# The first batch's attention norms by exp(ln(x)/2) from column sums held in every partition, scores scaled from PSUM in one pass, and v loaded behind the first weights

## The chip, the cores and the metric

The kernel runs on one core of a Trainium2 chip. The metric is the device time of one execution in microseconds. The kernel before took 830.83 us (median). TensorE is PE in the profile (PEld its weight loads), VectorE is DVE, ScalarE is ACT, GpSimd is POOL, SyncE is SP. SBUF and PSUM are the core's on-chip memories: in this kernel the tiles named ps_ lie in PSUM, the others in SBUF, and an "eviction" copies a matmul's result from a ps_ tile to SBUF.

## The reference

Four batches of cross-covariance attention over 6016 rows of 256 channels, and a gated feed-forward layer over all 24064 rows:

```python
qn = q / (norm(q, axis=1) + 1e-6);  kn = k / (norm(k, axis=1) + 1e-6)
a  = softmax(kn.T @ qn / tau)                     # 256 x 256 per batch, tau = 1
x  = (v @ a)                                      # 24064 x 256
out = (sigmoid(x @ w_gate) * (x @ w_val)) @ w_out # 256 -> 1536 -> 256
```

The kernel multiplies a into the weights first ("products" below: G = a·w_gate, H = a·w_val, twelve pieces of 128 x 512), so the large part of the work is v·G, v·H, their GLU (sigmoid of the gate half times the value half) and the product with w_out.

## The kernel before

For the first batch it streams q and k in, multiplies them into scores on TensorE, and sums squares for the norms. Then comes a stretch in which nothing large can run: norms, softmax, first products, first GLU step. This is the part that the change and the argument touch, with cuts (filler matmuls and arguments left out):

```python
for g, (t0, nt) in enumerate(groups0):      # stream of q and k
    ...                                     # squares, scores, norm sums as 4 columns
    norm_mms(ps_n0, ...)                    # sum of squares: q's 256 and k's 256 channels
norms_sqrt(0)                               # ScalarE: Sqrt of 128x4
nc.scalar.preload_act_table(ACT.Exp)
copy_s(0, 0); norms_inv(0); copy_s(0, 1)    # VectorE: +1e-6, reciprocal of 128x4; scores to SBUF
spread_k(0, 0, ...); spread_k(0, 1, ...)    # TensorE: k's inverse norms into every partition
weights(0, 0); weights(0, 1)                # VectorE product, ScalarE exponential, per 128x128
transpose_v(0, 0, ...)                      # first v group, TensorE, copied by VectorE and ScalarE
sums(0, 0); gh(0, 0, act=False); gh(0, 1, act=True)   # row sums; products, evicted by VectorE / ScalarE
sums(0, 1); gh(0, 2, act=False); gh(0, 3, act=True)
nc.scalar.preload_act_table(ACT.Sigmoid)
gh(0, 4, act=False)
# main loop: glu(b, ci, f), out_mms(...); side work in fixed slots, e.g.
at(7, lambda: transpose_v(0, 1, ...))       # second v group
```

Engines run their instructions in the order in which the program gives them. Later batches already compute their norms from k's sums in every partition, with a wide reciprocal, but beside the GLU of the batch before, where nobody waits for them.

Of the kernel before, what the change touches and what calls it, by code (L numbers as in the profile page):

```python
# [8 lines left out]

FP32 = mybir.dt.float32  # L10
BF16 = mybir.dt.bfloat16
# [6 lines left out]
def kernel(  # L18
# [20 lines left out]
    nc = tc.nc  # L39
# [47 lines left out]
    def mm(out, lhsT, rhs, start, stop, **kw):  # L87
        nc.tensor.matmul(out, lhsT=lhsT, rhs=rhs, start=start, stop=stop, **kw)  # L88
# [23 lines left out]
    first_f32 = [consts.tile([P, nt, C], FP32, name=f"first{w}") for w in range(2)]  # L112
    for eng, tl, src in zip((nc.sync, nc.scalar), first_f32, (q, k)):
        eng.dma_start(out=tl, in_=rows(src, 0)[:, t0 : t0 + nt, :])
    nc.scalar.preload_act_table(ACT.Sqrt)
    load_qk(0, *groups0[1])

    ident_bf = consts.tile([P, P], BF16)
    make_identity(nc, ident_bf)
    ident_f = consts.tile([P, P], FP32)  # L120
    make_identity(nc, ident_f)
    ones_bf = consts.tile([P, P], BF16)
    nc.vector.memset(ones_bf, 1.0)
    ones_wide = consts.tile([P, CH], BF16)
# [5 lines left out]
    nc.scalar.copy(qk[0, 0][1], first_f32[1])  # L130
    for t0, nt in groups0[2:]:
        load_qk(0, t0, nt)
    load_v(0, 0)

    w_sb = [[consts.tile([P, CB, FG], BF16, name=f"w_{n}{fg}") for fg in range(NFG)] for n in ("gate", "val")]
    w_out_sb = consts.tile([P, FC, C], BF16)
    for fg in range(NFG):
        for w, src in enumerate((moe_w_gate, moe_w_val)):
            nc.gpsimd.dma_start(  # L139
                out=w_sb[w][fg],  # L140
                in_=src.rearrange("(t p) f -> p t f", p=P)[:, :, ds(fg * FG, FG)],
            )
    load_v(0, 1)
    nc.gpsimd.dma_start(out=w_out_sb, in_=moe_w_out.rearrange("(t p) c -> p t c", p=P))

# [32 lines left out]
            )  # L178
        return sq

    def norm_mms(ps, sqs, nt, first, last, order=(0, 1)):

        for w in order:
            sq = sqs[w]
            for u in range(nt):
                for j in range(CB):
                    mm(
                        ps[:, w * CB + j : w * CB + j + 1],
                        sq[:, u, ds(j * P, P)],
                        ones_bf[:, 0:1],  # L190
                        start=(first and w == order[0] and u == 0 and j == 0),
                        stop=(last and u == nt - 1),
                        skip_group_check=True,
                    )

    def acc_start(b):
        st.setdefault(b, {})["acc"] = [
# [38 lines left out]
    def norms_mm(b):  # L236

        s = st[b]
        fold_q, fold_k = s["fold"]
        ps = psm.tile([P, CB + C], FP32, tag="m", name="ps_n")  # L240
        norm_mms(ps, (fold_q,), 2, True, True, (0,))
        for u in range(2):
            mm(ps[:, CB:], ones_bf, fold_k[:, u, :], False, u == 1, skip_group_check=True)
        s["n"] = ps

    def wide_sqrt(b):
# [25 lines left out]
                op1=ALU.mult,  # L272
            )

    def norms_sqrt(b):
        s = st[b]
        s["r"] = attp.tile([P, 2 * CB], FP32, tag="r", name="r")
        nc.scalar.activation(out=s["r"], in_=s["n"], func=ACT.Sqrt)

    def norms_inv(b):  # L280
        r = st[b]["r"]
        nc.vector.tensor_scalar(out=r, in0=r, scalar1=1e-6, scalar2=None, op0=ALU.add)
        nc.vector.reciprocal(r, r)
        if inv_tau != 1.0:
            nc.vector.tensor_scalar(
                out=r[:, :CB], in0=r[:, :CB], scalar1=inv_tau, scalar2=None, op0=ALU.mult
            )

    def spread_k(b, i, pl, tag):

        s = st[b]
        ps = pl.tile([P, P], FP32, tag=tag, name="ps_rk")
        mm(ps, s["r"][:, CB + i : CB + i + 1].to_broadcast([P, P]), ident_f, True, True)
        s.setdefault("rk", []).append(ps)

    def copy_s(b, j):
        s = st[b]
        if j == 0:
            s["x"] = attp.tile([P, CB, C], FP32, tag="x", name="x_sb")
        nc.vector.tensor_copy(out=s["x"][:, j, :], in_=s["s"][:, j, :])  # L300

    def weights(b, i):

        s = st[b]
        e = attp.tile([P, CB, P], BF16, tag=f"e{i}", name=f"e_sb{i}", bufs=2)
        for j in range(CB):
            y = attp.tile([P, P], FP32, tag=f"y{i}{j}", name="y_sb")
            nc.vector.tensor_tensor(
                out=y, in0=s["x"][:, j, ds(i * P, P)], in1=s["rk"][i], op=ALU.mult
            )  # L310
            nc.scalar.activation(
                out=e[:, j, :], in_=y, func=ACT.Exp, bias=shift, scale=s["r"][:, j : j + 1]
            )
        s.setdefault("e", []).append(e)
        s.setdefault("rrow", [])

# [39 lines left out]
            for n in ("G", "H")  # L356
        ]

    gh_order = [(fg, w, i) for fg in range(NFG) for i in range(CB) for w in range(2)]

    def gh(b, n, pl=None, tag=None, act=None):
        s = st[b]
# [17 lines left out]

    vts = {}

    def transpose_v(b, ci, ps=None, late=None):

        t0, nt = groups[ci]
        v_sb = vs.pop((b, ci))
        vT = vtpool.tile([P, TPC * CB, P], BF16, tag="vT", name="vT")
        flat = v_sb[:, :nt, :].rearrange("p t c -> p (t c)")
        if ps is None:
            nc.sync.dma_start_transpose(out=vT[:, : nt * CB, :], in_=flat)  # L390
        else:
            for n in range(nt * CB):
                nc.tensor.transpose(
                    out=ps[:, n, :], in_=flat[:, ds(n * P, P)], identity=ident_bf
                )
            half = nt * CB // 2
            nc.vector.tensor_copy(out=vT[:, :half, :], in_=ps[:, :half, :])
            (nc.scalar.copy if late is None else late)(vT[:, half : nt * CB, :], ps[:, half : nt * CB, :])
        vts[b, ci] = vT.rearrange("p (u cb) n -> p cb u n", cb=CB)

    hts = {}
# [70 lines left out]
            mm(ps, ones_bf, ones_wide, True, True)  # L472

    busy(9)
    ps_n0 = psm.tile([P, 2 * CB], FP32, tag="m", name="ps_n")

    n_acc = NT // TPC - 2
    acc_start(0)
# [2 lines left out]
    for g, (t0, nt) in enumerate(groups0):  # L481
        engines = (nc.vector, nc.scalar) if g < last0 else (nc.scalar, nc.vector)
        sq = [squares(0, t0, nt, w, engines[w], acc[w] if g == 0 else None) for w in range(2)]
        if 0 < g < n_acc:
            for w in range(2):
                nc.vector.tensor_tensor(out=acc[w], in0=acc[w], in1=sq[w], op=ALU.add)  # L486
        for u in range(nt):
            score(0, t0, u)
        if g < n_acc:
            busy(5)  # L490
        elif g == n_acc:
            norm_mms(ps_n0, acc, TPC, True, False)
            norm_mms(ps_n0, sq, nt, False, False)
        elif nt == TPC:
            busy(2)
            norm_mms(ps_n0, sq, nt, False, False)
        elif g < last0:
            held = (sq, nt)
        else:
            norm_mms(ps_n0, *held, False, False)  # L500
            norm_mms(ps_n0, sq, nt, False, True, (1, 0))
    st[0]["n"] = ps_n0
    norms_sqrt(0)
    nc.scalar.preload_act_table(ACT.Exp)
    copy_s(0, 0)
    norms_inv(0)
    copy_s(0, 1)
    busy(3)
    spread_k(0, 0, pso, "o")
    spread_k(0, 1, pso, "o")  # L510
    busy(1)
    weights(0, 0)
    weights(0, 1)
    late = []
    transpose_v(
        0, 0, psv.tile([P, TPC * CB, P], BF16, tag="v", name="ps_tp"), lambda *a: late.append(a)
    )
    nc.scalar.copy(*late.pop())
    gh_tiles(0)
    sums(0, 0)  # L520
    gh(0, 0, psg, "g", act=False)
    gh(0, 1, psv, "v", act=True)
    sums(0, 1, pss, "s")
    gh(0, 2, psg, "g", act=False)
    gh(0, 3, psv, "v", act=True)
    nc.scalar.preload_act_table(ACT.Sigmoid)
    gh(0, 4, pso, "o", act=False)


    def side_work(b):  # L530
# [7 lines left out]
        for ci in range(NCH):  # L538
            nb, nci = (b, ci + 1) if ci + 1 < NCH else (b + 1, 0)
            lb, lci = (b, ci + 2) if ci + 2 < NCH else (b + 1, ci + 2 - NCH)  # L540
            if (nb, nci) == (0, 1):
                at(7, lambda: transpose_v(0, 1, psm.tile([P, TPC * CB, P], BF16, tag="m", name="ps_tp")))
            elif nb < B:
                at(ci * FC + 2, transpose_v, nb, nci)
            if lb < B:
                at(ci * FC + 0, load_v, lb, lci)
# [33 lines left out]
    for b in range(B):  # L580
        side = side_work(b)
        for ci in range(NCH):
            block = b + 1 < B and ci in (9, 10)
            for f in range(FC):
                glu(b, ci, f)
                flush()
                if prev is not None and not block:
                    out_mms(*prev, f * TPC, (f + 1) * TPC)
                for fn, a in side.get((ci, f), ()):
                    fn(*a)  # L590
                if (b, ci) == (0, 0) and f < len(gh_order) - 5:
                    gh(0, 5 + f, pso, "o")
            if prev is not None and block:
                for s in range(TPC):
                    for fn, a in side.get((ci, FC + s), ()):
                        fn(*a)
                    out_mms(*prev, s * FC, (s + 1) * FC)
                    flush()
            prev = (b, ci)
# [39 lines left out]
```

## Time and profile before

| Kernel before | |
|---|---|
| time, median of 6 runs | 830.83 us (830.62 to 831.15) |
| span of the profiled run | 829.2 us |
| TensorE busy, 0 to 60 us | 16.01 + 16.30 + 19.08 of 60 us |
| first GLU step's matmuls | start 39.22 us |
| first product with w_out | starts 55.46 us |

The last two rows serve as marks below: from the first product with w_out on, TensorE has the same work in both kernels and hardly ever waits, so a difference at that mark should reappear at the end. In TensorE's timeline the mark is this line:

```profile
55.46 0.60 PE L88 MATMUL ps_o<-w_out_sb,hT 128*128 128x256 bf16 x4
```

The stretch between the last norm sum and the first exponentials, which the change replaces, reads as follows in ScalarE's and then VectorE's timeline of the kernel before (start us, length us, engine, line, operation, out<-in; in brackets the idle time before it and what ended it):

```profile
34.47 0.17 ACT L278 ACTIVATE r<-ps_n 128x4 f32<-128x4 f32 x1 [0.49 <-PE ps_n L88]
34.66 1.28 ACT L504 ACT_TABLE_LOAD   x1
36.02 1.65 ACT L311 ACTIVATE e_sb<-y_sb,shift,r 128x128 bf16<-128x128 f32 x4
...
34.87 0.18 DVE L283 RECIPROCAL r<-r 128x4 f32<-128x4 f32 x1
```

The reciprocal is of four columns (0.18 us), and the table load ends at 35.94.

### The profile page before, as it was taken

To read this page: it belongs to the slowest core of one execution; us is meant where nothing else is said; L and a number is where in the kernel's file an instruction comes from. 1 tells how busy PE (TensorE), PEld (TensorE's weight loads), DVE (VectorE), ACT (ScalarE), POOL (GpSimd) and SP (SyncE) were. 2 spreads that over 40 slices of the span, in tenths; PEclk is the share of its full clock that TensorE was granted. 3 is DMA by queue.
4 is the path that set the end of the run, shared out by engine and by line. 5 is a ranking of instruction groups with operands and counts; after the bars stand their busy time and mean duration, and the time that the engine had idled before them with its cause. 6 is when DMAs were issued, how large, how long until landed. Compare 5 with 4: busy or idle time off the path is not lost.

```text
span 829.2 us, 13794 instructions
## 1 busy us (share of the span) xinstructions
PE 816.6 (98%) x5204; PEld 502.9 (61%) x5218; DVE 588.7 (71%) x1023; ACT 391.6 (47%) x644; POOL 83.0 (10%) x159
## 2 busy tenths in 40 slices
PE   7899999999999999999999999999999999999998
PEld 4546666665666666665575666666566566666666
DVE  6577878787667777778767777777766666666665
ACT  4654444446644444445654444444655444444442
POOL 5532100002110100000211010000000000000000
PEclk9999999999999999999999999999999999999999
DMA  9999623226946433223875352223323423322111
GB/s 210 207 206 208 111 52 81 58 63 125 164 81 130 96 79 65 59 52 78 162 140 121 80 108 62 51 54 85 64 54 63 79 52 82 71 49 67 48 36 72
DMA packets 79028, 77.19 MB, mean 93 GB/s; under 512 B 50801, under 2 KB 55921, under 8 KB 78961
## 3 DMA queue, kind: packets, MB, share of 16 engines
q0 software_dynamic: 23920, 38.81, 28.1%
q1 hardware_dynamic: 54752, 36.91, 17.8%
q8 instruction: 41, 0.67, 0.3%
q10 hardware_dynamic: 288, 0.59, 0.2%
q14 instruction: 27, 0.21, 0.1%
HBM read 78.64 MB, written 24.64 MB: 125 GB/s over the span
## 4 chain that ended last, share of the span: by engine, by line
PE 94%; DMA 4%; DVE 1%; issue 0%; POOL 0%; ACT 0%; POOLq 0%; ACTq 0%
PE ps_o L88 30%; PE ps_gate L88 29%; PE ps_val L88 29%; PE ps_s L88 4%; DMA k_sb<-in_k_dram 3%; PE ps_gh L88 2%; DMA w_val<-in_moe_w_val_dram 1%; DVE hT L423 0%; ACT g_sb L422 0%; DVE sq L176 0%; PE ps_end L88 0%; POOL q_sb L97 0%; PE ps_n L88 0%; POOL w_gate L139 0%; POOL k_sb L97 0%
## 5 line engine op out<-in xcount | busy, mean ns | idle before, releaser
L423 DVE TENSOR_TENSOR hT<-ps_val,g_sb 128x512 bf16<-128x512 f32 (+1 forms) x576 | 390.9, 679 | 207.0 <-ACT g_sb L422 202.6
L422 ACT ACTIVATE g_sb<-ps_gate 128x512 bf16<-128x512 f32 (+1 forms) x576 | 338.2, 588 | 386.3 <-PE ps_gate L88 380.3
L88 PE MATMUL ps_gate<-vT,gh_G 128*128 128x512 bf16 (+1 forms) x1152 | 337.7, 375 | 0.6 <-ACT g_sb L422 0.4
L88 PE MATMUL ps_val<-vT,gh_H 128*128 128x512 bf16 (+1 forms) x1152 | 337.5, 375 | 0.4
L88 PE MATMUL ps_o<-w_out_sb,hT 128*128 128x256 bf16 x2244 | 324.8, 273 | 0.0
L88 PEld LDWEIGHTS <-hT 128*128 128x128 bf16 x2268 | 221.0, 98 | 124.6
L88 PEld LDWEIGHTS <-gh_H 128*128 128x128 bf16 x1152 | 112.7, 98 | 131.7 <-issue 1.4
L88 PEld LDWEIGHTS <-gh_G 128*128 128x128 bf16 x1152 | 112.4, 98 | 38.3 <-issue 0.6
L106 POOL DMA_DIRECT2D v_sb<-in_v_dram x48 | 25.5, 531 | 620.6 <-DMA vT<-v_sb 489.7
L449 DVE COPY out_sb<-ps_o 128x256 f32<-128x256 f32 x187 | 77.3, 413 | 12.6 <-PE ps_o L88 12.6
L88 PE MATMUL ps_s<-k_sb,q_sb 128*128 128x256 bf16 x376 | 66.0, 272 | 5.5 <-DMA k_sb<-in_k_dram 4.4
L88 PEld LDWEIGHTS <-q_sb 128*128 128x128 bf16 x376 | 36.6, 98 | 14.1 <-issue 6.8
L215 DVE TENSOR_TENSOR acc<-acc,sq 128x1024 bf16<-128x1024 bf16 (+1 forms) x66 | 44.1, 669 | 0.0
L176 DVE TENSOR_TENSOR sq<-q_sb 128x1024 bf16<-128x1024 bf16 (+2 forms) x44 | 29.4, 667 | 2.7 <-DMA q_sb<-in_q_dram 2.7
L97 POOL DMA_DIRECT2D q_sb<-in_q_dram x48 | 26.4, 551 | 16.5 <-DMA q_sb<-in_q_dram 8.3
L97 POOL DMA_DIRECT2D k_sb<-in_k_dram x48 | 26.3, 547 | 16.1 <-DMA k_sb<-in_k_dram 8.4
L176 DVE TENSOR_TENSOR sq<-k_sb 128x1024 bf16<-128x1024 bf16 (+2 forms) x34 | 22.4, 658 | 0.8 <-ACT sq L174 0.8
L376 ACT ACTIVATE gh_G<-ps_gh,rrow 128x512 bf16<-128x512 f32 x21 | 14.4, 687 | 12.9 <-PE ps_gh L88 9.1
L88 PE MATMUL ps_busy<-ones_wide,ones_bf 128*128 128x512 bf16 x57 | 16.6, 418 | 1.7 <-DVE shift L127 1.6
L174 ACT ACTIVATE sq<-k_sb 128x1024 bf16<-128x1024 bf16 (+1 forms) x11 | 11.2, 1018 | 14.7 <-DMA k_sb<-in_k_dram 11.9
L378 DVE TENSOR_SCALAR gh_H<-ps_gh,rrow 128x512 bf16<-128x512 f32 x22 | 16.3, 743 | 1.6 <-PE ps_gh L88 1.6
L486 DVE TENSOR_TENSOR acc<-acc,sq 128x1024 bf16<-128x1024 bf16 x16 | 11.1, 692 | 5.7 <-ACT sq L174 5.4
(67 smaller groups left out, 126.4 us busy)
## 6 DMA issues: line engine op xcount, KB each, us to landing
out_dram<-out_sb SPq DMA_DIRECT2D x44, 512.0 KB, 2.9
v_sb<-in_v_dram POOLq DMA_DIRECT2D x44, 256.0 KB, 3.8
q_sb<-in_q_dram POOLq DMA_DIRECT2D x43, 256.0 KB, 7.2
k_sb<-in_k_dram POOLq DMA_DIRECT2D x43, 256.0 KB, 8.1
out_dram<-out_sb SPq DMA_DIRECT2D x3, 384.0 KB, 2.5
w_gate<-in_moe_w_gate_dram POOLq DMA_DIRECT2D x3, 256.0 KB, 6.8
w_val<-in_moe_w_val_dram POOLq DMA_DIRECT2D x3, 256.0 KB, 8.1
w_out_sb<-in_moe_w_out_dram POOLq DMA_DIRECT2D x1, 768.0 KB, 12.7
```

What stands on the lines that cost most here:

```text
L88: nc.tensor.matmul(out, lhsT=lhsT, rhs=rhs, start=start, stop=stop, **kw)
L97: nc.gpsimd.dma_start(out=tl[:, :nt, :], in_=rows(src, b)[:, t0 : t0 + nt, :])
L106: nc.gpsimd.dma_start(out=v_sb[:, :nt, :], in_=rows(v, b)[:, t0 : t0 + nt, :])
L174: nc.scalar.activation(out=sq[:, :nt, :], in_=src[:, :nt, :], func=ACT.Square)
L176: engine.tensor_tensor(out=sq[:, :nt, :], in0=src[:, :nt, :], in1=src[:, :nt, :], op=ALU.mult)
L215: nc.vector.tensor_tensor(out=acc[:, :nt, :], in0=acc[:, :nt, :], in1=st[b]["sq", w][:, :nt, :], op=ALU.add)
L376: nc.scalar.activation(out=dst, in_=ps, func=ACT.Copy, scale=r)
L378: nc.vector.tensor_scalar(out=dst, in0=ps, scalar1=r, scalar2=None, op0=ALU.mult)
L422: nc.scalar.activation(out=g_sb[:, :n], in_=ps_gate[:, :n], func=ACT.Sigmoid)
L423: nc.vector.tensor_tensor(out=hts[b, ci][:, f, :n], in0=ps_val[:, :n], in1=g_sb[:, :n], op=ALU.mult)
L449: nc.vector.tensor_copy(out=out_sb[:, s, :], in_=ps)
L486: nc.vector.tensor_tensor(out=acc[w], in0=acc[w], in1=sq[w], op=ALU.add)
```

## The change

The intent is to shorten this stretch: one table set holds ln and exp, so the load between Sqrt and Exp falls away; the norms of k arrive already spread over all partitions, so the spreading matmuls fall away; the scores are scaled directly from PSUM. Along with it, the first v group is loaded behind the first weights, six products instead of five precede the main loop, the first transposes move behind two products, and the second transposes one slot (one step of the main loop) later with ScalarE's copy first. Later batches keep Sqrt. The core of the diff, with cuts and shortened lines:

```diff
-    nc.scalar.preload_act_table(ACT.Sqrt)
+    nc.scalar.add_instruction(mybir.InstLoadActFuncSet(...
+            act_func_set_id=list(get_activation_tables("trn2")).index("natural_log_exp_and_others")))
-    ident_f = consts.tile([P, P], FP32)
-    make_identity(nc, ident_f)
-    load_v(0, 0)
+        if fg == 0:                  # in the loop that loads the weights
+            load_v(0, 0)
     ...
+    def norm_k(ps, sq, nt, last, parts=1):      # k's sums: ones as weights, 256 columns
+                mm(ps[:, CB + i * n : CB + (i + 1) * n], ones_bf, sq[:, u, ds(i * n, n)], ...)
+    def roots(b, part):
+        nc.scalar.activation(out=x, in_=s["n"][:, cols], func=ACT.Ln)
+        nc.scalar.activation(out=x, in_=x, func=ACT.Exp, scale=0.5)
+    def weights(b, i):
+        wide_inv(b, i)                          # + 1e-6, reciprocal, of 130 or 128 columns
+        for j in range(CB):
+            nc.vector.scalar_tensor_tensor(out=y[:, j, :], in0=s["s"][:, j, ds(i * P, P)],
+                scalar=s["r"][:, j : j + 1], in1=s["rk"][:, ds(i * P, P)], op0=ALU.mult, op1=ALU.mult)
+        nc.scalar.activation(out=e, in_=y, func=ACT.Exp, bias=shift)
     ...
-    gh_order = [(fg, w, i) for fg in range(NFG) for i in range(CB) for w in range(2)]
+    gh_order = [(0, w, i) for i in range(CB) for w in range(2)]
+    gh_order += [(fg, w, i) for fg in range(1, NFG) for w in range(2) for i in range(CB)]
     ...
+            nc.scalar.copy(vT[:, half : nt * CB, :], ps[:, half : nt * CB, :])
             nc.vector.tensor_copy(out=vT[:, :half, :], in_=ps[:, :half, :])
-            (nc.scalar.copy if late is None else late)(vT[...], ps[...])
     ...
-    norms_sqrt(0) ... copy_s, norms_inv, spread_k, busy(3), busy(1), transpose_v(0, 0, ...)
+    for i in range(CB):
+        roots(0, i)
+    busy(8)
+    for i in range(CB):
+        weights(0, i)
     gh_tiles(0)
     sums(0, 0)
     gh(0, 0, psg, "g", act=False)
     gh(0, 1, psv, "v", act=True)
+    transpose_v(0, 0, psv.tile([P, TPC * CB, P], BF16, tag="v", name="ps_tp"))
     sums(0, 1, pss, "s")
     ...
     gh(0, 4, pso, "o", act=False)
+    gh(0, 5, pso, "o", act=False)
     ...
-                at(7, lambda: transpose_v(0, 1, ...))
+                at(8, lambda: transpose_v(0, 1, ...))
```

`busy(n)` is n filler matmuls that nobody reads; they keep TensorE working.

## The prediction

> **What bounds the kernel now.** I read the page first, then the busy time by stretches, the chain of work that ended last, the timeline of 28 to 54 us engine by engine, and the groups by form. The page says what fills the span:
>
> ```profile
> PE 816.6 (98%) x5204; PEld 502.9 (61%) x5218; DVE 588.7 (71%) x1023; ACT 391.6 (47%) x644; POOL 83.0 (10%) x159
> ...
> PE 94%; DMA 4%; DVE 1%; issue 0%; POOL 0%; ACT 0%; POOLq 0%; ACTq 0%
> ```
>
> TensorE carries 94% of the chain; everything else together is 6%. The busy time by stretches (columns: length, then busy us and count of PE, PEld, DVE, ACT, POOL, then clock, DMA share, GB/s) shows where that 6% lies:
>
> ```profile
> 0.00:20.00 20.00, 16.01 (x86) 8.95 (x88) 11.96 (x21) 8.67 (x8) 11.29 (x27) 1.00 1.00 210
> 20.00:40.00 20.00, 16.30 (x155) 10.34 (x157) 12.91 (x30) 11.42 (x17) 10.79 (x18) 1.00 1.18 206
> 40.00:60.00 20.00, 19.08 (x101) 9.52 (x101) 13.05 (x22) 12.63 (x21) 6.87 (x13) 1.00 1.20 206
> 60.00:70.00 10.00, 10.00 (x67) 6.29 (x66) 7.24 (x13) 4.18 (x7) 3.70 (x7) 1.00 1.13 197
> ```
>
> From 60 us on TensorE is simply full. Before that it isn't, and the DMA engines are saturated at a constant 206 to 210 GB/s. The change touches only this opening: the first batch's norms and softmax, the first loads, and two transposes of v. So whatever it does is decided before about 54 us, and every us by which TensorE reaches its full stretch earlier or later goes one to one into the end. Two stalls are left there, both seen in TensorE's timeline:
>
> ```profile
> 39.22 0.73 PE L88 MATMUL ps_gate<-vT,gh_G 128*128 128x512 bf16 x2
> 39.78 0.59 PE L88 MATMUL ps_val<-vT,gh_H 128*128 128x512 bf16 x2
> 40.75 0.59 PE L88 MATMUL ps_gh<-w_val,e_sb 128*128 128x512 bf16 x2 [0.37 <-DMA w_val<-in_moe_w_val_dram]
> ...
> 51.62 0.59 PE L88 MATMUL ps_val<-vT,gh_H 128*128 128x512 bf16 x2
> 52.58 0.59 PE L88 MATMUL ps_gate<-vT,gh_G 128*128 128x512 bf16 x2 [0.36 <-ACT g_sb L422]
> 53.31 0.59 PE L88 MATMUL ps_val<-vT,gh_H 128*128 128x512 bf16 x2
> ```
>
> Two 512-column matmuls take one step of 0.43 us (the starts lie that far apart when nothing waits). At 40.75 the sixth product with the weights waits for w_val of the second column group. After 51.62 + 0.43 = 52.05 two further pairs should have ended at 52.91; they end at 53.31 + 0.43 = 53.74, a loss of **0.83 us**. ScalarE's timeline has its cause:
>
> ```profile
> 51.44 0.58 ACT L398 COPY vT<-ps_tp 128x512 bf16<-128x512 bf16 x1 [1.19 <-DVE vT L397]
> 51.92 1.09 ACT L422 ACTIVATE g_sb<-ps_gate 128x512 bf16<-128x512 f32 x2
> ```
>
> ScalarE stood idle for 1.19 us until VectorE had copied its half of the transposed v, and the sigmoids queued behind.
>
> **What the Trainium skill says.** "ScalarE: Activation LUTs", section "Table sets: the hidden batching unit", states that natural_log_exp_and_others holds both exp and ln, so one load serves both; the change relies on it. Section "What ACT_TABLE_LOAD costs" gives about 1283 ns for a load and 186 ns + 0.833 ns per column for an activation without pointer operands. The trace agrees: loads last 1.28 us, and Sqrt of 128x258 took 388 ns against 401 by the formula. (The page adds a drain of about 1380 ns; here Sqrt ended at 34.64 and the load began at 34.66, so I don't count it.) "VectorE: DVE Perf Modes", section "First, the fixed hardware budget", says that Reciprocal is an iterative divide with a repeat count of 8. The trace agrees that it is slow per column, in the later batches, whose norms already have the wide form:
>
> ```profile
> L256 DVE RECIPROCAL n_sb<-n_sb 128x130 f32<-128x130 f32 x3 | 2.9, 966 | 0.1
> L256 DVE RECIPROCAL n_sb<-n_sb 128x128 f32<-128x128 f32 x3 | 2.9, 953 | 0.1
> L321 ACT ACTIVATE e_sb<-x_sb,shift 128x256 bf16<-128x256 f32 x6 | 2.7, 500 | 0.7 <-DVE x_sb L266 0.7
> L266 DVE SCALAR_TENSOR_TENSOR x_sb<-ps_s,n_sb 128x256 f32<-128x256 f32 x6 | 2.6, 474 | 0.0
> ...
> L283 DVE RECIPROCAL r<-r 128x4 f32<-128x4 f32 x1 | 0.2, 178 | 0.0
> ```
>
> "PSUM — Partial Sum Buffer", section "PSUM bank collisions raise a hardware error", says accesses of two engines to one bank must be guarded by bank, reads against reads too. The wait of ScalarE's copy above fits that: its half is another column range of the same tile.
>
> **The change part by part.** *Transfers.* The stream to the last k is the same bytes; the last k lands at 27.11 + 6.5 = 33.6 us as before. v and the first two weight tiles only swap places. Removing the second identity lets GpSimd issue about half a us earlier at 3 us, but the DMA engines are full from there on: 0. The second w_val still lands at 40.7, and the new order asks for it after six products and two GLU steps, so the 0.37 us wait goes, provided the rest isn't later anyway.
>
> *Norm sums.* In the last full group 8 one-column matmuls (16 take 33.34 - 32.93 = 0.41 us, so 0.2) become 4 of 256 columns (0.108 each, 0.43): +0.23. The held and last groups cost 0.35 + 0.17 against 0.30 to 0.35. The last sum ends near 34.85 instead of 34.43: **+0.4**.
>
> *Roots to exponentials.* Before: Sqrt at 34.47, reciprocal of four columns done at 35.05, spreading matmuls, products; the first pair of exponentials done about 36.9, the second at 37.67. After, each a step with 0.03 us between dependents: Ln at 34.90, Ln and Exp of 130 columns 0.28 each (formula above, checked on Sqrt), end 35.49. VectorE: add 0.22, reciprocal **0.97**, two scalings of 128 columns (estimate from 474 ns for 256: 0.34, starts 0.26 apart) 0.60; end 37.37. Exponential 0.50: first half done 37.92. Second half on VectorE: add to 37.50, reciprocal to 38.48, scalings to 39.11, exponential to **39.65**. That is 1.0 us later for the first half and 2.0 for the second. The saved table load of 1.28 us (34.66 to 35.94) was only just binding before, the first exponential having followed at 36.02; it buys little because two reciprocals of 0.96 take its place.
>
> *From there to the first GLU.* VectorE reaches the row sums only after the second half's scalings: inverse at 39.37, first eviction 39.40 to 40.14. ScalarE evicts its first to 40.25, copies its v half to 40.74; VectorE's half follows (same bank) to 41.19, second inverse 41.50, second gate eviction 42.27. ScalarE's second value eviction ends 42.22, the Sigmoid load 43.52, the first sigmoid 44.12. TensorE meanwhile does six products and the transposes, then the first GLU step ends at 42.95. The third step's value matmuls wait about 0.2 us for VectorE to release the first value tile (44.12 + 0.72 = 44.84). Before, TensorE had done the same set of work at 40.75 + 0.43 = 41.18. So TensorE is 42.95 + 0.2 - 41.18 = **+1.97 us** late; the w_val wait of before is already inside this difference.
>
> *Transposes of the second v group* one step later, after the products are over, with ScalarE's copy first: the copy starts as soon as the transposes end, and the next sigmoid slips by a few tenths, within the slack of the two gate buffers. The stall goes: **-0.83**.
>
> Sum: +1.97 - 0.83 = +1.14. From 54 us on nothing differs: 830.83 + 1.14 = **832.0 us**.
>
> **Rivals.** *The chain of before was worse than its parts, and the change gains.* If the reciprocals lay beside something else, losing the load and both stalls would give about -0.83 - 0.37 - 0.2, near 829.5. Against it: VectorE's order is fixed, and the first exponential needs the reciprocal's columns. *The head is hidden by the transfers.* If TensorE waited for weights anyway, the later exponentials would cost nothing and only the second stall's 0.83 would show: 830.0. For it: the chain runs through w_val to 40.71. Against it: after that time TensorE would still lack its evicted weights until 42.27. *Extra loads.* If a load of another set is put before Ln or Exp, +1.3 to +2.6 us, 833.3 to 834.6; the explicit load of a set with both speaks against it. *The transposes stall again* in the new place: 832.8.
>
> **Range and chances.** My main term is a chain of some fifteen durations, each from a row, with about 0.5 us of error in how they are queued; the stall that goes may be worth 0.3 to 1.2. That makes 830.6 to 833.1 for 8 in 10, the lower end reaching towards the hidden-head rival. Two per cent is 16.6 us, more than everything that the change touches could give or take: faster 0.005, same 0.99, slower 0.005.
>
> **What would show it.** Right: no table load between the first Ln and the last Exp; two reciprocals near 0.96 us ahead of the first batch's exponentials; the second exponential ending near 39.6; the first gate matmuls waiting for VectorE's eviction until past 42; no gap in TensorE around 50 to 56. Wrong: exponentials done before 38, or a first GLU step under way by 40, would mean the chain was mis-sized and the kernel is faster; a gap after the second transposes would put it near 832.8.

## The result, and the profile after

The changed kernel takes **833.25 us** (median of 6 runs, 832.65 to 833.39), 2.42 us more than the 830.83 us of before. The ratio is 1.0027 (95% interval 1.0015 to 1.0040), within 2% and yet clear of the noise. Ratios here are the mean time of one kernel's fast runs over that of the other's fast runs of the same rounds, so they are not quite the ratio of the medians quoted. The median lies 0.15 us above the top of the predicted range: the direction was right, and twice as much was lost as the sum said.

First the busy line and the chain line of the page after, and below them the busy time by stretches, in the columns explained in the prediction:

```profile
PE 818.4 (98%) x5191; PEld 503.9 (61%) x5204; DVE 591.0 (71%) x1023; ACT 390.6 (47%) x644; POOL 82.6 (10%) x157
...
PE 95%; DMA 3%; DVE 1%; issue 0%; ACT 0%; POOL 0%; DVEq 0%; POOLq 0%
```

```profile
20.00:40.00 20.00, 15.28 (x130) 10.05 (x131) 12.21 (x24) 8.07 (x13) 10.79 (x18) 0.99 1.18 206
40.00:60.00 20.00, 19.78 (x100) 9.37 (x99) 15.22 (x25) 13.84 (x23) 6.87 (x13) 0.92 1.20 206
```

From 20 to 40 us TensorE is busy 1.0 us less than before, and from 40 to 60 it is busy 0.7 us more, but at a granted clock of 0.92 where it had 1.00: part of that busy time is slow time, not more work. The chain through the norms, in VectorE's timeline of the changed kernel:

```profile
35.46 0.74 DVE L273 TENSOR_SCALAR n_sb<-n_sb 128x130 f32<-128x130 f32 x1 [1.44 <-ACT n_sb L302]
36.24 0.97 DVE L274 RECIPROCAL n_sb<-n_sb 128x130 f32<-128x130 f32 x1
37.32 0.61 DVE L310 SCALAR_TENSOR_TENSOR y_sb<-ps_s,n_sb 128x128 f32<-128x128 f32 x2
37.84 0.22 DVE L273 TENSOR_SCALAR n_sb<-n_sb 128x128 f32<-128x128 f32 x1
38.10 0.95 DVE L274 RECIPROCAL n_sb<-n_sb 128x128 f32<-128x128 f32 x1
39.09 0.61 DVE L310 SCALAR_TENSOR_TENSOR y_sb<-ps_s,n_sb 128x128 f32<-128x128 f32 x2
```

VectorE works without a pause from 35.46 to 39.70, and 1.92 us of it are the two reciprocals. The first addition of 1e-6 stands out: 0.74 us, where the second, almost as wide, takes 0.22. ScalarE, between its last root and the exponentials, waits:

```profile
37.97 0.51 ACT L319 ACTIVATE e_sb<-y_sb,shift 128x256 bf16<-128x256 f32 x1 [2.02 <-DVE y_sb L310]
39.73 0.51 ACT L319 ACTIVATE e_sb<-y_sb,shift 128x256 bf16<-128x256 f32 x1 [1.26 <-DVE y_sb L310]
```

The exponentials end at 38.48 and 40.24; before, the last one ended at 36.02 + 1.65 = 37.67. TensorE's timeline from the filler matmuls to the first GLU step:

```profile
34.61 1.89 PE L89 MATMUL ps_busy<-ones_wide,ones_bf 128*128 128x512 bf16 x8
38.53 0.20 PE L89 MATMUL ps_r<-ones_bf,e_sb 128*128 128x1 bf16 x2 [2.03 <-ACT e_sb L319]
...
39.45 0.92 PE L400 MATMUL ps_tp<-ident_bf,v_sb 128*128 128x128 bf16 x8
...
42.03 1.51 PE L89 MATMUL ps_gh<-w_gate,e_sb 128*128 128x512 bf16 x4
43.38 0.59 PE L89 MATMUL ps_gate<-vT,gh_G 128*128 128x512 bf16 x2
```

TensorE idles from 36.50 to 38.53. A first look would stop there, but the lengths say more: eight transposes take 0.92 us (0.61 in the kernel before), and four 512-column matmuls 1.51 us (1.02 in e7 below). The busy time of a finer cut shows why (third column from the end is the clock):

```profile
39.50:41.50 2.00, 1.78 (x13) 1.09 (x13) 1.36 (x5) 1.56 (x3) 0.67 (x2) 0.52 1.23 208
41.50:43.00 1.50, 1.50 (x5) 0.57 (x4) 1.22 (x4) 0.71 (x2) 0.54 (x2) 0.50 1.24 202
43.00:45.00 2.00, 2.00 (x11) 0.92 (x10) 1.51 (x3) 1.98 (x3) 0.74 (x2) 1.00 1.46 197
```

For about 3.4 us TensorE ran at half its clock. It isn't an accident of the profiled run: the mean clock of all six runs of the changed kernel is 0.997 to 0.999. Half a clock lost for 3.4 of 831 us is 0.002. The one round with 0.999 is the fastest of the six (832.65 us). A mean of 0.998 also stands in two of the 18 later rounds of the kernel before (832.18 and 832.67 us) and in one of e2; where in those rounds it was low isn't known, as their traces weren't kept.

At the second transposes, where the kernel before lost 0.83 us, TensorE now goes on without a gap (each start is the one before plus 0.43, or 0.45 on either side of the transposes); the last line is the mark:

```profile
53.31 0.62 PE L89 MATMUL ps_val<-vT,gh_H 128*128 128x512 bf16 x2
53.76 0.61 PE L400 MATMUL ps_tp<-ident_bf,v_sb 128*128 128x128 bf16 x8
54.21 0.59 PE L89 MATMUL ps_gate<-vT,gh_G 128*128 128x512 bf16 x2
...
57.66 0.60 PE L89 MATMUL ps_o<-w_out_sb,hT 128*128 128x256 bf16 x4
```

The first product with w_out starts at 57.66, 2.20 us later than before; the span is 2.1 us longer. Nearly all of the difference is there at that mark.

### The profile page after: what moved, and what is told of

It reads as the page before. It is cut to its first block, busy times and chain, and to the rows that moved or that the text cites. A ratio compares the mean times of both kernels' runs of the same rounds, so it can differ in the third digit from the quotient of the medians.

```text
span 831.3 us, 13764 instructions
## 1 busy us (share of the span) xinstructions
PE 818.4 (98%) x5191; PEld 503.9 (61%) x5204; DVE 591.0 (71%) x1023; ACT 390.6 (47%) x644; POOL 82.6 (10%) x157
## 4 chain that ended last, share of the span: by engine, by line
PE 95%; DMA 3%; DVE 1%; issue 0%; ACT 0%; POOL 0%; DVEq 0%; POOLq 0%
PE ps_o L89 29%; PE ps_gate L89 29%; PE ps_val L89 29%; PE ps_s L89 4%; DMA k_sb<-in_k_dram 3%; PE ps_gh L89 3%; DVE hT L430 0%; PE ps_n L89 0%; DVE sq L183 0%; PE ps_end L89 0%; ACT g_sb L429 0%; PE ps_tp L400 0%; DVE n_sb L274 0%; POOL q_sb L98 0%; DVE n_sb L273 0%
## 5 line engine op out<-in xcount | busy, mean ns | idle before, releaser
L89 PEld LDWEIGHTS <-e_sb 128*128 128x128 bf16 x112 | 10.4, 101 | 7.6 <-ACT e_sb L319 2.7
L89 PE MATMUL ps_gh<-w_val,e_sb 128*128 128x512 bf16 x45 | 14.1, 390 | 0.4 <-issue 0.2
```

Of the source, the lines that this page charges most:

```text
L89: nc.tensor.matmul(out, lhsT=lhsT, rhs=rhs, start=start, stop=stop, **kw)
```

## The experiments

Eight kernels ran on the chip, each with five timed rounds beside the kernel before (medians 830.78 us); all gave correct results. The mark is the start of the first product with w_out in the profiled run. The changed kernel wasn't timed again. It was run at another time. The ratios' intervals are about 1 us wide to each side: by them the changed kernel, e2, e7 and e8 are slower than the kernel before, e5 and e6 faster, and e1, e3 and e4 not told apart from it.

| Kernel | median us | ratio to before (95%) | mark us |
|---|---|---|---|
| before | 830.83 | 1 | 55.46 |
| changed | 833.25 | 1.0027 (1.0015 to 1.0040) | 57.66 |
| e1: changed, exp(-ln(x)/2), no reciprocals | 830.56 | 0.9994 (0.9981 to 1.0006) | 54.87 |
| e2: changed, 17 filler matmuls | 832.91 | 1.0024 (1.0011 to 1.0036) | 57.17 |
| e3: before, second transposes of the change | 829.88 | 0.9989 (0.9975 to 1.0002) | 54.12 |
| e4: all of the change but the norms | 830.78 | 0.9997 (0.9984 to 1.0009) | 55.03 |
| e5: e1, row sums early, v copy later | 829.89 | 0.9987 (0.9974 to 0.9999) | 54.08 |
| e6: e1, v transposed in the gap | 829.52 | 0.9984 (0.9971 to 0.9996) | 53.99 |
| e7: changed, w_out issued later | 832.36 | 1.0017 (1.0004 to 1.0030) | 56.86 |
| e8: e2 and e7 together | 832.34 | 1.0018 (1.0004 to 1.0032) | 56.76 |

My theory after the result: the wide reciprocals in the chain cost most of the time; two things that I hadn't counted, the blocked addition and the slow clock, cost the rest. The rivals: the new order of products and copies costs it; the slow clock lies in slack; the addition waits for ScalarE.

### e1: without the reciprocals

```diff
-        nc.scalar.activation(out=x, in_=x, func=ACT.Exp, scale=0.5)
+        nc.scalar.activation(out=x, in_=x, func=ACT.Exp, scale=-0.5)
 ...
     def weights(b, i):
-        wide_inv(b, i)
```

exp(-ln(x)/2) is the inverse norm at once. (The 1e-6 is left out, and 1/tau with it, which is 1 here; a channel of zeros would not be survived.)

> The changed kernel with exp(-ln(x)/2) in place of exp(ln(x)/2), so that the sum of 1e-6 and the reciprocal fall away for the first batch (the result differs by about 1e-7). Main theory (the two wide reciprocals of 0.97 and 0.95 us in the chain cost the time): the second half's exponentials end near 37.2 us instead of 40.2, TensorE no longer idles 2 us, its clock stays at 1.00, the first product with w_out starts near 55.0 us instead of 57.66, and the time is near 830.2 us, 3 us under the changed kernel. Rival (the order of the evictions and of the transposes costs it, the reciprocals lie beside other work): at most 0.5 us better than the changed kernel, so 832.7 or more.

Measured: 830.56 us, 2.7 us under the changed kernel. In e1's profile VectorE makes all four scalings in one go, and ScalarE both exponentials:

```profile
35.50 1.13 DVE L309 SCALAR_TENSOR_TENSOR y_sb<-ps_s,n_sb 128x128 f32<-128x128 f32 x4 [1.44 <-ACT n_sb L302]
36.14 1.02 ACT L318 ACTIVATE e_sb<-y_sb,shift 128x256 bf16<-128x256 f32 x2 [0.17 <-DVE y_sb L309]
```

They end at 37.16, as expected, and the clock stays at 1.00. The rival that the order costs it all falls: with the order unchanged, taking the additions and reciprocals out removes the loss (how much of it is the blocked addition, e7 shows).

### e2: more filler

```diff
-    busy(8)
+    busy(17)
```

> The changed kernel with 17 filler matmuls instead of 8 before the first products, so that TensorE works until about 38.3 us instead of idling from 36.5. Theory (the idle 2 us let the granted clock fall to 0.5 from 39.6 to 43, and that held the first GLU step until 43.38): the clock stays at 1.00, the first GLU step starts when the second gate eviction ends, near 42.9, the first product with w_out near 57.1, and the time falls by 0.5 us to about 832.7. Rival (TensorE would have waited for the evictions anyway, the slow clock lies in slack): within 0.1 us of the changed kernel, 833.2.

Measured: 832.91 us, the clock of the profiled run 1.00 throughout, the mark 57.17, 0.49 us earlier; the medians differ by 0.34 us. The timed rounds of the two kernels overlap, and so do the ratios' intervals; what speaks clearer are the spans, 830.8 to 831.0 in all five rounds, against 831.2 to 831.3 in five of the changed kernel's six and 830.7 in the sixth, the one with a clock of 0.999. So the slow clock wasn't all in slack, and the theory holds, a little smaller than I said. The first GLU step now waits for an eviction (the bracket), exactly at the 42.9 expected:

```profile
42.17 0.38 PE L89 MATMUL ps_gate<-vT,gh_G 128*128 128x512 bf16 x1
42.94 0.39 PE L89 MATMUL ps_gate<-vT,gh_G 128*128 128x512 bf16 x1 [0.39 <-DVE gh_G L385]
```

### e3: only the second transposes

```diff
-            nc.vector.tensor_copy(out=vT[:, :half, :], in_=ps[:, :half, :])
             (nc.scalar.copy if late is None else late)(vT[:, half : nt * CB, :], ps[:, half : nt * CB, :])
+            nc.vector.tensor_copy(out=vT[:, :half, :], in_=ps[:, :half, :])
 ...
-                at(7, lambda: transpose_v(0, 1, ...))
+                at(8, lambda: transpose_v(0, 1, ...))
```

> The kernel before with only the transposes of the second v group one step later and ScalarE's copy ahead of VectorE's. Theory (a stall of 0.83 us is taken away): no gap in TensorE between 50 and 54, the first product with w_out at 54.6 instead of 55.46, time 830.0 us. Rival (the stall comes back at the new place, or the time is taken back later): 830.6 to 830.9.

Measured: 829.88 us, 0.9 us under the kernel before. ScalarE's copy now begins 0.3 us after its last sigmoid, not 1.19, and the next sigmoid follows at 51.34:

```profile
50.86 0.58 ACT L397 COPY vT<-ps_tp 128x512 bf16<-128x512 bf16 x1 [0.30 <-PE ps_tp L393]
```

The mark moved by 1.34 us, more than the 0.83 counted. That profile has the sixth product at 40.20 instead of 40.75, since the second w_val happened to land earlier (7.5 us after its issue, not 8.1); from the sixth product to the mark it is 54.12 - 40.20 = 13.92 us, before 55.46 - 40.75 = 14.71, so the transposes are worth 0.79. The wait for w_val is thus not the same in every execution, with the same order of loads.

### e4: everything but the norms

The kernel before with the new load order, product order, place of the first transposes, and e3's edit; norms_sqrt, norms_inv, spread_k and the old weights stay (diff as in "The change", without its norm parts).

> All of the change but the norms: order of the loads, order of the products, transposes, but the square roots, four-column reciprocal and spreading matmuls of the kernel before. Main theory (the norms alone make it slower): no reciprocal of 0.9 us before the first products, the first product with w_out near 55.0, time near 830.3 us, which is 3 us under the changed kernel. Rival (the new order of products and copies costs it): 832 us or more.

Measured: 830.78 us, so the norms alone are worth 833.25 - 830.78 = 2.5 us of loss. But the expected 830.3 isn't quite reached, and against e3 in the same rounds e4 is 0.9 us slower: the new order costs what the second transposes gain. VectorE's timeline of e4 says how:

```profile
39.19 0.42 DVE L400 COPY vT<-ps_tp 128x512 bf16<-128x512 bf16 x1 [0.86 <-ACT vT L399]
...
39.99 2.07 DVE L380 TENSOR_SCALAR gh_G<-ps_gh,rrow 128x512 bf16<-128x512 f32 x3
```

VectorE stands 0.86 us waiting for ScalarE's half of v, because in its order this copy comes ahead of the second row sums and the second gate eviction. In the kernel before that copy was long done. The three evictions from 39.99 could have begun earlier.

e1 against e4 also tells what the new norms are worth with no reciprocals: 830.56 against 830.78, 0.2 us, which is within the scatter of their rounds (830.14 to 830.73 and 830.61 to 830.86). Saving the table load and the spreading matmuls buys that little at most.

### e5: row sums ahead of the transposes

```diff
-    transpose_v(0, 0, psv.tile([P, TPC * CB, P], BF16, tag="v", name="ps_tp"))
     sums(0, 1, pss, "s")
+    transpose_v(0, 0, psv.tile(...), late)      # VectorE's copy is held back
     gh(0, 2, psg, "g", act=False)
+    nc.vector.tensor_copy(**late.pop())
```

(on top of e1)

> The kernel of e1_neg with the second half's row sums ahead of the transposes and VectorE's v copy behind the second gate eviction. Theory (once the reciprocals are gone, the wait of VectorE for ScalarE's v copy, 0.86 us in e1_neg, is what holds the second gate eviction and the first GLU step): the second gate eviction ends near 39.5 us instead of 40.56, the gate matmul's wait of 0.39 us is gone, the first product with w_out starts near 54.1 instead of 54.87, time near 829.8 us. Rival (the products or the Sigmoid load hold TensorE anyway): no change against e1_neg, 830.5.

Measured: 829.89 us, 0.67 us under e1, mark 54.08 (0.79 earlier, 0.18 of it because Ln started at 34.66 and not 34.84 in this run). The second gate eviction starts at 38.58 now and waits only for its product:

```profile
38.58 0.75 DVE L384 TENSOR_SCALAR gh_G<-ps_gh,rrow 128x512 bf16<-128x512 f32 x1 [0.34 <-PE ps_gh L89]
```

So the cost of the order is the place of VectorE's copy, as e4 suggested.

### e6: v ahead of the weights again

On top of e1, with load_v(0, 0) ahead of the weights as before, and

```diff
-    busy(8)
+    busy(1)
+    transpose_v(0, 0, psv.tile(...), late)      # both copies held back
+    busy(5)
     for i in range(CB):
         weights(0, i)
+    VectorE's copy; ScalarE's copy
```

> The kernel of e1_neg with v loaded ahead of the first weights again and transposed while TensorE waits for the exponentials, as in the kernel before; its copies behind the scalings and exponentials. Theory (0.45 us of transposes leave the full stretch of TensorE, and the copies leave the way of the evictions): the first product with w_out near 53.9 us, time near 829.6 us, under both kernels by 1.2 and 3.6 us. Rival (the first w_val lands near 37.4 us and holds the second product, and the copies delay the row sums): 830.2 or more.

Measured: 829.52 us, mark 53.99: the best of all, 1.3 us under the kernel before and 3.7 us under the changed one. Part of the rival is seen too: the second product starts at 37.38, not 0.43 but 0.62 after the first at 36.76, about when the w_val of the first column group lands in this order of loads (issued at 30.55, landed 6.8 us later).

### e7: w_out issued later

GpSimd's longest issue, that of w_out, ran beside the slow addition. GpSimd's timeline of the changed kernel:

```profile
35.11 1.05 POOL L151 DMA_DIRECT2D w_out_sb<-in_moe_w_out_dram  x1
```

```diff
-    nc.gpsimd.dma_start(out=w_out_sb, in_=moe_w_out.rearrange("(t p) c -> p t c", p=P))
+    def load_w_out(): ...                       # the same, called in slot 0 of the main loop,
+                at(0, load_w_out)               # behind the first q and k of the next batch
```

> The changed kernel with the load of w_out issued after the first q and k of the next batch, so that GpSimd isn't issuing for 1.05 us (35.11 to 36.16) while VectorE adds 1e-6 to the first half's roots; the next v load is then issued from 35.1 to 35.65. Theory (the addition took 0.74 us instead of 0.22 because it waited for GpSimd's long issue to end): it takes about 0.4 us, everything after it is 0.3 us earlier, time about 833.0. Rival (it waits for ScalarE's last exponential of the roots at 35.94, or is slow for itself): it still takes 0.74 us and ends 0.26 us after that exponential.

Measured: 832.36 us, 0.9 us under the changed kernel. The addition takes 0.27 us and ends at 35.91, before ScalarE's last root does (35.80 + 0.31 = 36.11), so it never waited for that:

```profile
35.64 0.27 DVE L275 TENSOR_SCALAR n_sb<-n_sb 128x130 f32<-128x130 f32 x1 [1.44 <-ACT n_sb L304]
35.80 0.31 ACT L304 ACTIVATE n_sb<-n_sb 128x128 f32<-128x128 f32 x1
...
38.22 0.20 PE L89 MATMUL ps_r<-ones_bf,e_sb 128*128 128x1 bf16 x2 [1.55 <-ACT e_sb L321]
```

It gained more than the 0.3 us expected. The chain is 0.5 us shorter, not 0.3, since I had expected the addition to be held for 0.2 us by the next issue; and TensorE's idle time shrank from 2.03 to 1.55 us, after which the clock stayed at 1.00. One edit took away both unforeseen terms. (e7's rounds, 832.24 to 832.63, don't overlap those of the changed kernel, 832.65 to 833.39.)

### e8: e2 and e7 together

> The changed kernel with both the 17 filler matmuls and the later load of w_out. Theory (the idle clock and the blocked addition are what the prediction missed): the first product with w_out near 56.8 us, time about 832.5, near the predicted 832.0. Rival (they don't add, as the evictions set the pace in both): 832.9, as with the filler matmuls alone.

Measured: 832.34 us, mark 56.76; e7 alone has 832.36. With the clock already held by the shorter idle time, the filler had nothing left to do. This is the changed kernel as I had imagined it, without the blocked addition and the slow clock, and it lies 0.3 us above the predicted 832.0.

## Why the prediction was right or wrong

**Transfers: right.** The last k lands as before, and the DMA engines move 206 GB/s from 20 to 60 us in both. The wait for w_val is gone.

**Norm sums: right.** Ln started at 34.81, Sqrt before at 34.47, with the stream 0.1 us earlier this time (the last full group's scores started at 31.53 instead of 31.63), so 0.44 for +0.4.

**Roots to exponentials: the mechanism right, one term mis-sized.** Ln and Exp took 0.28 and 0.31 us, the reciprocals 0.97 and 0.95, the pairs of scalings 0.61, the exponentials 0.51, each within 0.03 of what was counted. The step that failed is "add 0.22" in the first half: it measured 0.74. The second half's exponential therefore ended at 40.24, not 39.65. That GpSimd's issue was the cause is shown by e7, and again by e8 (0.26 us). The Trainium skill, "SBUF — State Buffer", section "Who interferes with whom", names the mechanism: VectorE and GpSimd share a pair of SBUF ports as an exclusive lock, a tensor_scalar can take it, and the later of the two blocks fully. The trace fits: the addition, which began after the issue, ended 0.04 us after the issue's recorded end of 36.16; in e7 it ended 0.06 after the loads of v that GpSimd then issued until 35.85. The other direction isn't seen: the issue of 37.88, begun 0.04 us after the second addition, took 0.53 us, as it did in e1 with no addition there. No run here separates the port from another tie between the two.

**From there to the first GLU: a term is missing.** "The first GLU step ends at 42.95" became 43.81 + 0.43 = 44.24, 1.29 us later. From the blocked addition, the second gate eviction came 0.59 us later (42.11 + 0.75 = 42.86 instead of 42.27). Nearly all of the rest is the clock: the transposes and the last four of the six products ran at half speed until 43, which put the end of the first step 0.65 us behind that of e2 (43.16 + 0.43 = 43.59). The Trainium skill, "TensorE: Matmul & The Clock Gate", section "What's actually happening", describes a gate that halves the clock after idle time and lifts it after sustained work, on a free-running window of about 3.4 us. The trace agrees in kind (0.50 for 3.4 us), not in the length of idle that it takes (last section). I had read the granted clock of 1.00 in the kernel before and not asked what an idle stretch of my own making, 36.5 to 37.9 in my working, would do to it. As far as e7 shows, those 1.4 us would have been harmless (1.55 us were); the blocked addition made them 2.03. So one step stands behind both misses, "add 0.22", and without its delay the kernel took 832.36 (e7), within the predicted range. The 0.2 us wait at the third step didn't show in the changed kernel, for TensorE was late enough (it shows in e2, where a value pair starts at 45.49, 0.60 after the gate pair and not 0.43). So +1.97 became 44.24 - 41.18 = +3.06.

**Transposes of the second v group: right.** -0.83 was counted; from the end of the first step's set (41.18, 44.24) to the mark it is 14.28 us before and 13.42 after, -0.86. e3 shows it by itself.

**Sum:** +3.06 - 0.86 = +2.20 at the mark, 2.1 in the span, 2.4 in the medians, against +1.14. Of the rivals, the gain, the hidden head, the extra loads and a new stall at the transposes are out. What I didn't separate is the price of the new order of copies: it was inside my working, but only e4 and e5 show that it is 0.7 to 0.9 us and avoidable.

## What to carry to other kernels

Widening an operand from 4 to 130 columns to save a spreading step is free only for operations that cost little per column; price each of them from a row of the same width, the reciprocal first, and see whether exp(-ln(x)/2) makes it unnecessary. In a stretch where TensorE waits, ask two more questions than the durations answer: what GpSimd is issuing beside VectorE's SBUF operations, and how long TensorE idles. And where two engines share the eviction of one PSUM tile, put the second copy in that engine's order only where it would wait for nothing.

## What the Trainium skill lacked or had wrong

- "TensorE: Matmul & The Clock Gate": its table lets the clock fall after at least one idle window of about 3.4 us. Here 2.03 us of idle were followed by a clock of 0.5 from about 39.6 to 43.0, 3.1 us after the idle began and a good 1 us after work had resumed, while 1.55 us in e7, a kernel different in one load, had no such effect, nor had 1.68 us ahead of 7.13 in e2. The state came back after about 3.4 us, as the page says.
- "ScalarE: Activation LUTs": besides the 1283 ns of a table load it counts a drain of about 1380 ns per switch. No such drain stands in these traces: the load of 42.98 + 1.28 us was followed by the first sigmoid at 44.27.
- "VectorE: DVE Perf Modes": it says that a reciprocal iterates 8 times and gives no duration. Here it took 178 ns for 4 columns and 966 ns for 130, which is (966 - 178) / 126 = 6.3 ns per column, while the addition of the same 130 columns took 219 ns in the later batches.
- "SBUF — State Buffer": its rule on the shared ports agrees with the runs where VectorE came second; the size that it has for a GpSimd load issue in a short chain, 0.52 us for one addition, stands on no page.
